# Six banks of batch 1's first DFT stage by sums and differences in a spectral filter with a gated MLP

## The chip, the cores and the metric

The kernel runs on one core of a Trainium2 chip. A core has TensorE (PE in the profile; its weight loads are the row PEld), VectorE (DVE), ScalarE (ACT), GpSimd (POOL) and SyncE (SP), which here only issues DMAs. Sixteen DMA engines move data between HBM and the core's SBUF, whose 128 partitions hold the operands; matmul results go to PSUM, which has eight banks of 128 partitions by 512 fp32 numbers. The metric is the time of one execution on the device in microseconds.

## What is computed

```
x: (8, 3008, 256) fp32     filt: (1505, 256) complex, given as two fp32 arrays
X = rfft(x, axis=1)                      # along the 3008 positions of a batch
y = irfft(X * filt, n=3008, axis=1)      # a global filter
out = (relu(y @ w_gate) * (y @ w_val)) @ w_out
w_gate, w_val: (256, 1536)   w_out: (1536, 256)   out: (24064, 256) fp32
```

The 24,064 tokens are the positions of the eight batches. The MLP is by far the larger part of the arithmetic; the transforms are written as matmuls too.

## The kernel before

**The transform.** A batch's 3008 positions are a grid of 94 (n1) by 32 (n2, here called the columns). The forward transform has two stages. Stage A is a DFT over n1: for each column, 94 input rows times a table of cosines and sines, WA. Stage 2 (`fwd`, L395) is a DFT over the columns, with 64x32 tiles of TensorE side by side. Its result is multiplied by the real and by the imaginary part of the filter (`product`, L411: `tt` with Ftr, `uu` with Fti), and `inv` (L437) transforms back over the columns. A last matmul, `item_c` (L555), goes back over n1 and yields y transposed (psY, then yT in bf16), as the MLP needs it.

**The MLP.** Tokens are worked in 47 blocks of 512. `gv` (L573) makes, for one of 12 slices of the hidden width, the value and the gate by two bf16 matmuls each (psV, psG), ACT copies psV, and DVE forms relu(gate) times value. `o_part` (L591) multiplies by w_out for the block before. The main loop runs over the blocks and slices; the transforms of the later batches are hung onto its steps by hand (`at_step`, L701). The order of work on every engine is the order in which the program is written.

**The prologue.** Before the first gv, batch 0 must be transformed and filtered; `first_b` (L474) does that in steps, and while its DVE and ACT work goes on, stage A of batch 1 fills TensorE. This stage A has 16 banks: each is one fp32 matmul (`a_bank`, L262, shown at L267) of the whole table WA, 128x128, by four columns and one half of the 256 channels, 512 numbers. The fp32 matmul shows as two records in the profile. `a_1` (L282) calls it and has ACT drain the bank: channels' first half (h = 0) in one copy into a part of dCb named AS1[0], the second half (h = 1) in two copies into two buffers with the tag "asb", of which the pool has three. The order of the 16 banks is a plain list: groups p of eight columns, halves h, four columns s within the group (L670). `first_b` takes two of them at each of three stops (`item(2)`), the third just ahead of `inv(0, 2)`, the last part of batch 0's inverse transform over the columns. Then follow in the text: the loads of the MLP's weights, issued by POOL (`load_vg`, L245, `load_o`, L250); the table M1; the two transposes `turn_d` on DVE (L318, shown at L302), which turn batch 0's result into the form that psY reads; `item(7)`; the psY matmuls of the first block; `item(3)`; and the main loop.

**Loads of batch 1.** SP issues twelve DMAs (`load_x`, L187, shown at L192) behind a small one that holds the queue until the filter is there. Each carries 32 (or 30) rows of n1 and eight columns, 8 KB a row. Row i of chunk m goes into partition m + 4 i, so one DMA spreads over all 128 partitions. The columns come in order; XF[0] holds columns 0 to 15, XF[1] 16 to 31.

**Other steps that the text below speaks of.** `store_half` (L323) and `load_half` (L329) send the h = 0 half of stage A's result through HBM, once its last bank is drained; `turn_1` (L309) turns the h = 1 half on DVE. The products of batch 0 are split: for i = 0, 1, 2 and e = 1 POOL makes them, from a copy `xs` that ACT takes out of PSUM (L421, L422), the rest are made by DVE (L424). PSUM banks are handed out from a list in the order in which they were given back (`bank`, L149), so the order of the text decides which bank, and so which wait, a matmul meets. The last POOL operation of the prologue multiplies Fti by plus and minus one (L694).

Of the kernel before, what the change touches and what calls it, by code (L numbers as in the profile page):

```python
# [12 lines left out]
FP32 = mybir.dt.float32  # L13
BF16 = mybir.dt.bfloat16
ALU = mybir.AluOpType
# [14 lines left out]
N1, N2 = 94, 32  # L30
# [86 lines left out]
def kernel(  # L117
# [10 lines left out]
    nc = tc.nc  # L128
# [9 lines left out]
    assert NB * W == B * S  # L138

    wa_h, fold_h, f2_h, tab_h = _tables()  # L140

    ctx.enter_context(tc.manual_schedule())
    consts = ctx.enter_context(tc.tile_pool(name="consts", bufs=1))
# [12 lines left out]
    def done(t):  # L156
        free.append(held.pop(id(t))[0])
# [7 lines left out]
    XF = [consts.tile([128, NX2 * D], FP32, name=f"XF{c}") for c in range(N2 // NX2)]  # L165
    XP = [t[:, i * 2048:i * 2048 + 2048].rearrange("p (k d) -> p k d", d=512) for t in XF for i in range(2)]
    WA = pro.tile([128, 128], FP32)
    AS0 = pro.tile([128, 4, N2 // 2, D // 8, 4], BF16)
    DS0 = AS0.rearrange("p q n c f -> p (q n c f)").rearrange("p (k c f) -> p k c f", c=D // 2, f=4)
    dCb = consts.tile([128, 48, D], BF16)  # L170
# [1 line left out]
    AS1 = [dCb[:, 32:48, :].rearrange("p n d -> p (n d)").rearrange("p (l c d) -> p l c d", l=NC2, d=D // 2)]  # L172
    WF = consts.tile([128, 4, 32], FP32)
    M1 = consts.tile([128, 2, N1], BF16)
    F2 = consts.tile([128, NG, 64], BF16)
    I2t = consts.tile([128, 2, NG // 2, 64], BF16)
    I2u = pro.tile([128, 2, NG // 2, 64], BF16)
# [101 lines left out]
            nc.scalar.copy(dst[:, :, q.start + i], src[:, :, i])  # L279
        done(psA)  # L280

    def a_1(p, s, h):  # L282

        psA = a_bank(NC2 * p + 4 * s, 4, h * D // 2, D // 2)
        if h and len(AS1) == 1:
            for _ in range(2):
                t = sb.tile([128, NC2 * D], BF16, tag="asb", bufs=3, name="asb")
                AS1.append(t.rearrange("p (l c d) -> p l c d", l=NC2, c=N2 // NC2))
        ts = AS1[1:] if h else AS1[:1]
        w = D // 2 // len(ts)  # L290
        for i, t in enumerate(ts):
            nc.scalar.copy(t[:, 4 * s:4 * s + 4, p, :], psA[:, :, i * w:(i + 1) * w])
        done(psA)

    def turn_a(dst, src):

# [66 lines left out]
    def tiled_a(b, j):  # L363

        banks = [bank("psF", 2, D) for _ in range(4)]
        for c in range(4):
            for q in range(4):
                r = 32 * q
                nc.tensor.matmul(banks[q][32 * c:32 * c + 32], WF[r:r + 24, c, :],  # L369
                                 fold[b, j][c][r:r + 24], start=True, stop=True,  # L370
                                 tile_position=(r, 32 * c))
        asf = sb.tile([128, NC2 * D], BF16, tag="asb", bufs=3, name="asb")
        asf = asf.rearrange("p (n q d) -> p n q d", n=2, d=D)
        for q in range(4):
            copy = nc.scalar.copy if q % 2 == 0 else nc.vector.tensor_copy
            copy(asf[:, :, q, :], banks[q])  # L376
            done(banks[q])
        for c in range(4):
            rr = 2 * (1 - c // 2) + c % 2
            nc.sync.dma_start(_ap(Abuf[b], (rr * N2 + 8 * j) * NG * D, [[D, NG], [NG * D, 8], [1, D]]),  # L380
                              asf[32 * c:32 * c + NG].rearrange("p n q d -> p (n q) d"))
# [5 lines left out]
            nc.sync.dma_start(ats[b][:, 8 * z:8 * z + 8].rearrange("p j d -> p (j d)"),  # L387
                              _ap(Abuf[b], 8 * z * D, [[NG * D, 128], [1, 8 * D]]))

    ON_POOL = ((0, 1), (1, 1), (2, 1))  # L390
    ats = {}

    psXs, tus, left, xs = {}, {}, {}, {}
# [43 lines left out]
    def inv(b, q):  # L437

        psD = [bank("psD", 2, D) for c in range(4)]
        last = 0 if b else 1  # L440
        for m in range(2):
            for k in range(last + 1):
                for r in range(2):
                    for c in range(4):
                        for e in range(2):
                            i = 2 * q + m
                            nc.tensor.matmul(psD[c][64 * e:64 * e + 64, m],  # L447
                                             (I2t, I2u)[k][32 * c:32 * c + 32, r, 2 * i + e, :],
                                             tus[b, i, e, k][32 * c:32 * c + 32, r],
                                             start=(k == r == 0), stop=(k == last and r == 1),  # L450
                                             tile_position=(32 * c, 64 * e))
        dst = sb.tile([128, 8, D], BF16, tag="dsb", bufs=3, name="dsb") if b else DS0
        def out(cs):
            for c in cs:
                copy = nc.vector.tensor_copy if (c % 2 if b else (q, c) in ((1, 3), (2, 0), (2, 1))) else nc.scalar.copy
                if b:
                    copy(dst[:, c:8:4, :], psD[c])
                else:
                    k, g = 4 * q + c // 2, c % 2 * 2
                    copy(dst[:, k:k + 3:2, :, g:g + 2], psD[c].rearrange("p m (f e) -> p m e f", f=2))  # L460
                done(psD[c])
        if not b:
            return out(range(4))

        def rest():
            out((2, 3))
            for z in range(4):
                nc.sync.dma_start(_ap(Dbuf[b], (64 * (z // 2) + z % 2) * NG * D + 8 * q * D,
                                      [[2 * NG * D, 32], [1, 8 * D]]),
                                  dst[32 * z:32 * z + 32])  # L470
        out((0, 1))
        return rest

    def first_b(item):  # L474

        def products(i, es=(1, 0)):
            for e in es:
                for k in range(2):
                    product(0, i, e, k, pool=(i, e) in ON_POOL)

        for i in range(3):
            fwd(0, i)
            if i < 2:
                products(i)
        make_back_u()
        products(2)
        warm(3)
        fwd(0, 3)
        products(3, (1,))
        warm(3)  # L490
        fwd(0, 4)
        item(2)
        products(3, (0,))
        inv(0, 0)
        fwd(0, 5)
        products(4)
        item(2)
        products(5)
        place_own()
        inv(0, 1)  # L500
        item(2)
        inv(0, 2)

    dCs = {}
# [161 lines left out]
            warm(4)  # L666
    hold = sb.tile([2, 8], BF16, tag="hold", bufs=1)
    nc.sync.dma_start(hold, Ftr[0:2, 4, 0:8])
    load_x(1, sp, ((0, 0, 2 * q), (0, 2 * q, 4 * q), (1, 0, 2 * q), (1, 2 * q, 4 * q)))
    items = iter([(p, s, h) for p in range(4) for h in range(2) for s in range(2)])  # L670

    def item(n):
        for _ in range(n):
            p, s, h = next(items)
            a_1(p, s, h)
            if (p, s, h) == (3, 1, 0):
                new_at(1)
                store_half(1)
                load_half(1)

    first_b(item)
    load_vg(0, DFF // 2)
    load_vg(DFF // 2, DFF)
    load_o()
    nc.gpsimd.tensor_copy(M1, tabs[:, 578:].rearrange("p (l n) -> p l n", l=2))
    for h in range(2):
        turn_d(h)
    item(7)
    for m in range(y_items(0)):
        for h in range(2):  # L690
            item_c(m, h)
    item(3)
    turn_1(0)
    nc.gpsimd.tensor_scalar(Fti, Fti, conj[:, 0:1], 1.0, op0=ALU.mult, op1=ALU.mult)  # L694
# [90 lines left out]
```

## Time and profile before

| What | Value |
|---|---|
| median of three runs | 865.34 us (863.85, 865.34, 865.4) |
| profiled execution, its own time | 863.39 us |
| its span | 861.6 us |
| PE busy | 853.8 us |
| DVE, ACT, POOL busy | 578.6, 500.2, 458.0 us |
| first gv matmul (psV) | 45.85 us |
| twelve loads of batch 1, issued | 20.84 to 29.89 us |

The busy times are sums over the span of one execution. A row of a timeline gives the start and the length in us, the engine, the line, the operation, the tiles it writes and reads with partitions and sizes, and how many instructions were taken together; in brackets stands the idle time ahead of it and what ended it. The windows give for each stretch of time the busy time and the number of instructions of PE, PEld, DVE, ACT and POOL, then TensorE's granted clock, the busy share of the DMA engines and their GB/s; a share can pass 1 a little, since packets of an engine overlap at their ends. Times of moments are counted from the start of the span.

### The profile page before, as it was taken

The page shows a single profiled execution, that of the slowest core. Times are in us where ns is not written, and L with a number is a line of the kernel's source. Part 1 is how long each engine was busy: PE and PEld are TensorE (multiplying, and loading weights), DVE is VectorE, ACT ScalarE, POOL GpSimd, SP SyncE. Part 2 cuts the span into 40 slices and gives each one's busy share as a digit, 9 for nine tenths or more (in the row PEclk, how much of TensorE's full clock was granted, in tenths as well). Part 3 has the DMA queues.
Part 4 walks back from the last instruction along what each step waited for, and adds up shares of the span by engine and source line. Part 5 has one row for each costly group of instructions (what it writes and reads, how often), then busy time and mean ns, then how long its engine had stood idle before and what let it go on. Part 6 is the DMA issues. An engine that isn't in the chain of part 4 may idle for free.

```text
span 861.6 us, 20366 instructions
## 1 busy us (share of the span) xinstructions
PE 853.8 (99%) x7614; PEld 497.3 (58%) x7614; DVE 578.6 (67%) x864; ACT 500.2 (58%) x944; POOL 458.0 (53%) x494
## 2 busy tenths in 40 slices
PE   9999999999999999999999999999999999999997
PEld 4456655656556555665556665565655656666665
DVE  3878865777657876577765787658766578555554
ACT  5765565556655565555655565655565555565552
POOL 6747890488986765776667756867550033000001
PEclk9999999999999999999999999999999999999999
DMA  9995375333762339534294333842454222511112
GB/s 248 239 166 124 98 156 145 104 113 106 195 190 79 80 92 190 175 84 102 73 211 153 99 101 94 201 147 77 103 118 119 97 62 51 129 39 31 37 32 55
DMA packets 102862, 101.60 MB, mean 118 GB/s; under 512 B 21703, under 2 KB 89959, under 8 KB 101995
## 3 DMA queue, kind: packets, MB, share of 16 engines
q1 hardware_dynamic: 83407, 77.93, 34.1%
q0 software_dynamic: 18848, 21.68, 11.6%
q8 instruction: 60, 0.98, 0.5%
q10 hardware_dynamic: 508, 0.68, 0.3%
q14 instruction: 39, 0.32, 0.1%
HBM read 58.23 MB, written 45.88 MB: 121 GB/s over the span
## 4 chain that ended last, share of the span: by engine, by line
PE 98%; DMA 1%; SPq 1%; issue 0%; ACT 0%; DVE 0%
PE psV L578 29%; PE psO L599 29%; PE psG L578 28%; PE psF L369 3%; PE psA L267 3%; PE psY L561 3%; PE psD L447 2%; PE psX L404 1%; DMA XF<-in_x_dram 1%; SPq L192 1%; PE psI L209 0%; ACT AS L460 0%; DVE XF L608 0%; SPq L637 0%
## 5 line engine op out<-in xcount | busy, mean ns | idle before, releaser
L583 DVE SCALAR_TENSOR_TENSOR prod<-psG,vsb 128x512 bf16<-128x512 f32 x564 | 389.5, 691 | 234.0 <-ACT vsb L581 229.9
L581 ACT CAST vsb<-psV 128x512 bf16<-128x512 f32 x564 | 332.4, 589 | 217.6 <-PE psV L578 210.2
L599 PE MATMUL psO<-WoT,prod 128*128 128x256 bf16 x2256 | 336.5, 273 | 0.0
L578 PE MATMUL psV<-yT,WvT 128*128 128x512 bf16 x1128 | 336.2, 380 | 0.0
L578 PE MATMUL psG<-yT,WgT 128*128 128x512 bf16 x1128 | 335.3, 379 | 0.0
L599 PEld LDWEIGHTS <-prod 128*128 128x128 bf16 x2256 | 220.7, 98 | 143.4
L578 PEld LDWEIGHTS <-WgT 128*128 128x128 bf16 x1128 | 110.0, 97 | 133.9 <-issue 1.1
L434 POOL TENSOR_TENSOR pp<-tt,uu 128x256 bf16<-128x256 f32 x84 | 61.1, 727 | 169.8 <-DVE uu L424 159.9
L578 PEld LDWEIGHTS <-WvT 128*128 128x128 bf16 x1128 | 100.4, 98 | 36.9 <-issue 25.6
L569 ACT CAST yT<-psY 128x470 bf16<-128x470 f32 (+16 forms) x134 | 58.8, 457 | 46.6 <-PE psY L561 46.5
L608 ACT COPY osb<-psO 128x512 f32<-128x512 f32 x92 | 53.9, 586 | 25.2 <-PE psO L599 24.1
L621 POOL DMA_DIRECT2D out_dram<-osb x5 | 2.6, 539 | 119.2 <-ACT osb L608 117.7
L424 DVE TENSOR_TENSOR tt<-psX,Ftr 128x512 f32<-128x512 f32 (+1 forms) x93 | 63.5, 683 | 0.5 <-PE psX L404 0.5
L424 DVE TENSOR_TENSOR uu<-psX,Fti 128x512 f32<-128x512 f32 (+1 forms) x93 | 63.3, 681 | 0.2 <-DMA Fti<-in_filt_i_dram 0.2
L435 POOL TENSOR_TENSOR pp<-tt,uu 128x256 bf16<-128x256 f32 x84 | 61.0, 726 | 0.0
L355 POOL TENSOR_TENSOR fold<-XF 128x1024 f32<-128x1024 f32 x24 | 56.5, 2352 | 4.8 <-DMA XF<-in_x_dram 4.3
L356 POOL TENSOR_TENSOR XF<-XF 128x1024 f32<-128x1024 f32 x24 | 56.5, 2355 | 1.9
L259 POOL CAST scr<-prod 128x8 f32<-128x8 bf16 x19 | 3.6, 192 | 85.7 <-DVE prod L583 85.7
L342 POOL DMA_DIRECT2D XF<-in_x_dram x76 | 45.7, 604 | 2.1 <-issue 1.0
L376 DVE CAST asb<-psF 128x512 bf16<-128x512 f32 x48 | 30.9, 686 | 17.7 <-PE psF L369 17.7
L376 ACT CAST asb<-psF 128x512 bf16<-128x512 f32 x48 | 25.8, 589 | 28.9 <-PE psF L369 28.9
L561 PE MATMUL psY<-M,dCb 96*128 96x94 bf16 (+2 forms) x514 | 39.9, 205 | 0.0
(68 smaller groups left out, 456.4 us busy)
## 6 DMA issues: line engine op xcount, KB each, us to landing
Dbuf<-dsb SPq DMA_DIRECT2D x84, 128.0 KB
dCb<-Dbuf SPq DMA_DIRECT2D x56, 192.0 KB
XF<-in_x_dram POOLq DMA_DIRECT2D x38, 256.0 KB, 7.4
Abuf<-asb SPq DMA_DIRECT2D x96, 96.0 KB
at<-Abuf SPq DMA_DIRECT2D x18, 512.0 KB
XF<-in_x_dram SPq DMA_DIRECT2D x31, 256.0 KB
XF<-in_x_dram POOLq DMA_DIRECT2D x76, 96.0 KB, 5.2
out_dram<-osb SPq DMA_DIRECT2D x69, 94.0 KB
```

What stands on the lines that cost most here:

```text
L355: tt(t, xp[:, 0:2], xp[:, 2:4], op=ALU.add)
L356: tt(xp[:, 2:4], xp[:, 0:2], xp[:, 2:4], op=ALU.subtract)
L376: copy(asf[:, :, q, :], banks[q])
L424: nc.vector.tensor_tensor(p, psX, filt, op=ALU.mult)
L434: nc.gpsimd.tensor_tensor(p[:, 0], tt[:, 0], uu[:, 1], op=ALU.subtract)
L435: nc.gpsimd.tensor_tensor(p[:, 1], tt[:, 1], uu[:, 0], op=ALU.add)
L561: nc.tensor.matmul(psY[:, o:o + w], d_rows(b, col, h), M1[:, 1, n1:n1 + w] if b == 0 else M1[:NROW, 0, n1:n1 + w], start=True, stop=True)
L569: copy(yT[:, h, p:p + w], psY[:, o:o + w])
L578: nc.tensor.matmul(pt[:, :W], w[:, h, ft * 128:(ft + 1) * 128], yT[:, h, y0:y0 + W], start=(h == 0), stop=(h == 1))
L581: nc.scalar.copy(vsb, psV[:, :W])
L583: nc.vector.scalar_tensor_tensor(prod, in0=psG[:, :W], scalar=0.0, in1=vsb, op0=ALU.max, op1=ALU.mult)
L599: nc.tensor.matmul(psO[:, t % 2], prods[ft][:, t * 128:(t + 1) * 128], WoT[:, ft, :], start=(ft == 0), stop=(ft == NFT - 1))
```

## The change

Stage A of batch 1 is done in three ways. Columns 0 to 7 and 24 to 31 stay as they were, eight banks. Columns 8 to 23 are loaded otherwise: four DMAs (`load_halves`) bring them in runs of eight columns, with the rows n1 = 0 to 47 in one half (k = 0) and 47 to 94 in the other (k = 1), columns 8 to 15 into partitions 0 to 47, columns 16 to 23 into partitions 64 to 111. Of those eight banks, six are done from sums and differences: POOL forms row n1 plus row n1 + 47 and row n1 minus row n1 + 47, four adds in all (`fold_halves`), and `a_halves` multiplies the sum by the columns of the table that it needs and the difference by the others, with four fp32 matmuls on four 64x64 tiles for two banks. The last two (`a_halves(1, 1)`) are done without sums, as two accumulating steps over the two halves of n1. A new table WH holds the parts of WA in that arrangement.

With it come smaller ones. The buffers "asb" are four, not three. In `first_b` the products of i = 0, 1, 2 are written with three tt ahead of three uu on DVE, and POOL's in the order tt, tt, uu, uu, tt, uu. The third stop in `first_b` takes one bank, not two; ahead of psY stand `a_halves(1, 1)`, one plain bank and three `a_halves` with sums, and behind it two plain banks, not three. The first plain bank after columns 0 to 7 is one of columns 24 to 27, which come with the last three loads. One AS copy of `inv(0, 1)` moves from ACT to DVE. On POOL the adds, M1 and a small copy of a sign column stand between the halves of the weight loads, and the multiplication of Fti comes after the last of them. On SP there are eleven DMAs for batch 1 instead of twelve: three `load_x`, four `load_halves`, WH, three `load_x`.

```diff
+    wh_h = np.zeros((128, 2, 128), np.float32)
+    n1 = np.arange(N1).reshape(2, N1 // 2)
+    for r in (0, 64):
+        wh_h[r:r + N1 // 2] = wa_h[n1 % 32 * 4 + n1 // 32].transpose(1, 0, 2)
...
-    def a_1(p, s, h):
-
-        psA = a_bank(NC2 * p + 4 * s, 4, h * D // 2, D // 2)
+    def out_1(psA, n2, h):
+
         if h and len(AS1) == 1:
             for _ in range(2):
-                t = sb.tile([128, NC2 * D], BF16, tag="asb", bufs=3, name="asb")
+                t = sb.tile([128, NC2 * D], BF16, tag="asb", bufs=4, name="asb")
...
+    XH = [XF[k][:, NC2 * D * (1 - k):NC2 * D * (2 - k)] for k in range(2)]
+
+    def load_halves(b):
+
+        for k in range(2):
+            for r in range(2):
+                nc.sync.dma_start(XH[k][64 * r:64 * r + 48],
+                                  _ap(x, ((b * N1 + N1 // 2 * k) * N2 + NC2 * (1 + r)) * D,
+                                      [[N2 * D, 48], [1, NC2 * D]]))
+
+    def cols_h(k, s, d0, nd):
+
+        return XH[k].rearrange("p (n d) -> p n d", d=D)[:, 4 * s:4 * s + 4, d0:d0 + nd]
+
+    def fold_halves(s, d0, nd):
+
+        lo, hi = (cols_h(k, s, d0, nd) for k in range(2))
+        t = pro.tile([128, 4, nd], FP32, tag=f"sum{s}", name="sum")
+        nc.gpsimd.tensor_tensor(t, lo, hi, op=ALU.add)
+        nc.gpsimd.tensor_tensor(hi, lo, hi, op=ALU.subtract)
+        for h in range(d0 * 2 // D, (d0 + nd) * 2 // D):
+            sums[s, h] = t[:, :, h * D // 2 - d0:h * D // 2 - d0 + D // 2]
+
+    def a_halves(s, h):
+
+        banks = [bank("psA", 4, D // 2) for _ in range(2)]
+        lo, hi = (cols_h(k, s, h * D // 2, D // 2) for k in range(2))
+        if (s, h) in sums:
+            jobs = [(64 * e, 64, 0, src, True, True) for e, src in ((1, sums[s, h]), (0, hi))]
+        else:
+            jobs = [(0, 128, k, src, k == 0, k == 1) for k, src in enumerate((lo, hi))]
+        for c, w, k, src, start, stop in jobs:
+            for r in (0, 64):
+                nc.tensor.matmul(banks[r // 64][c:c + w], WH[r:r + N1 // 2, k, c:c + w], src[r:r + N1 // 2],
+                                 start=start, stop=stop, tile_position=(r, c))
+        for r in range(2):
+            out_1(banks[r], NC2 * (1 + r) + 4 * s, h)
...
-                copy = nc.vector.tensor_copy if (c % 2 if b else (q, c) in ((1, 3), (2, 0), (2, 1))) else nc.scalar.copy
+                copy = nc.vector.tensor_copy if (c % 2 if b else (q, c) in ((1, 2), (1, 3), (2, 0), (2, 1))) else nc.scalar.copy
...
         for i in range(3):
             fwd(0, i)
-            if i < 2:
-                products(i)
+        for k in range(2):
+            for i in range(2):
+                product(0, i, 1, k, pool=True)
+        for i in range(3):
+            product(0, i, 0, 0)
         make_back_u()
-        products(2)
+        for k in range(2):
+            product(0, 2, 1, k, pool=True)
+        for i in range(3):
+            product(0, i, 0, 1)
...
-        item(2)
+        item(1)
         inv(0, 2)
...
-    load_x(1, sp, ((0, 0, 2 * q), (0, 2 * q, 4 * q), (1, 0, 2 * q), (1, 2 * q, 4 * q)))
-    items = iter([(p, s, h) for p in range(4) for h in range(2) for s in range(2)])
+    load_x(1, sp, ((0, 0, 2 * q),))
+    load_halves(1)
+    nc.sync.dma_start(WH, nc.inline_tensor(wh_h, name="dft_wh").ap())
+    load_x(1, sp, ((1, 2 * q, 4 * q),))
+    items = iter([(n2, h) for p in (0, 3) for h in range(2) for n2 in (NC2 * p, NC2 * p + 4)])
...
     first_b(item)
     load_vg(0, DFF // 2)
+    fold_halves(0, 0, D)
+    nc.gpsimd.tensor_copy(M1, tabs[:, 578:].rearrange("p (l n) -> p l n", l=2))
+    nc.gpsimd.tensor_copy(sign, conj[:, 0:1])
+    fold_halves(1, 0, D // 2)
     load_vg(DFF // 2, DFF)
     load_o()
-    nc.gpsimd.tensor_copy(M1, tabs[:, 578:].rearrange("p (l n) -> p l n", l=2))
+    nc.gpsimd.tensor_scalar(Fti, Fti, sign, 1.0, op0=ALU.mult, op1=ALU.mult)
     for h in range(2):
         turn_d(h)
-    item(7)
+    a_halves(1, 1)
+    item(1)
+    for s, h in ((0, 0), (0, 1), (1, 0)):
+        a_halves(s, h)
+    new_at(1)
+    store_half(1)
+    load_half(1)
     for m in range(y_items(0)):
         for h in range(2):
             item_c(m, h)
-    item(3)
+    item(2)
     turn_1(0)
-    nc.gpsimd.tensor_scalar(Fti, Fti, conj[:, 0:1], 1.0, op0=ALU.mult, op1=ALU.mult)
```

More of the change, by code (lines that the diff above doesn't have):

```diff
@@ L167 @@
     WA = pro.tile([128, 128], FP32)
+    WH = pro.tile([128, 2, 128], FP32)
     AS0 = pro.tile([128, 4, N2 // 2, D // 8, 4], BF16)
@@ L174 @@
     M1 = consts.tile([128, 2, N1], BF16)
+    sign = consts.tile([128, 1], BF16)
     F2 = consts.tile([128, NG, 64], BF16)
@@ L290, in a_1 @@
         w = D // 2 // len(ts)
+        l, p = n2 % NC2, n2 // NC2
         for i, t in enumerate(ts):
-            nc.scalar.copy(t[:, 4 * s:4 * s + 4, p, :], psA[:, :, i * w:(i + 1) * w])
+            nc.scalar.copy(t[:, l:l + 4, p, :], psA[:, :, i * w:(i + 1) * w])
         done(psA)
+    def a_1(n2, h):
+        out_1(a_bank(n2, 4, h * D // 2, D // 2), n2, h)
+    XH = [XF[k][:, NC2 * D * (1 - k):NC2 * D * (2 - k)] for k in range(2)]
[5 more added lines that the diff above has]
+                                      [[N2 * D, 48], [1, NC2 * D]]))
+    sums = {}
+    def cols_h(k, s, d0, nd):
[20 more added lines that the diff above has]
+            out_1(banks[r], NC2 * (1 + r) + 4 * s, h)
     def turn_a(dst, src):
@@ L371, in tiled_a @@
                                  tile_position=(r, 32 * c))
-        asf = sb.tile([128, NC2 * D], BF16, tag="asb", bufs=3, name="asb")
+        asf = sb.tile([128, NC2 * D], BF16, tag="asb", bufs=4, name="asb")
         asf = asf.rearrange("p (n q d) -> p n q d", n=2, d=D)
@@ L388, in load_at_tiled @@
                               _ap(Abuf[b], 8 * z * D, [[NG * D, 128], [1, 8 * D]]))
-    ON_POOL = ((0, 1), (1, 1), (2, 1))
     ats = {}
@@ L478, in products @@
                 for k in range(2):
-                    product(0, i, e, k, pool=(i, e) in ON_POOL)
+                    product(0, i, e, k)
         for i in range(3):
             fwd(0, i)
-            if i < 2:
-                products(i)
+        for k in range(2):
[3 more added lines that the diff above has]
+            product(0, i, 0, 0)
         make_back_u()
-        products(2)
+        for k in range(2):
+            product(0, 2, 1, k, pool=True)
+        for i in range(3):
+            product(0, i, 0, 1)
         warm(3)
@@ L668 @@
     nc.sync.dma_start(hold, Ftr[0:2, 4, 0:8])
-    load_x(1, sp, ((0, 0, 2 * q), (0, 2 * q, 4 * q), (1, 0, 2 * q), (1, 2 * q, 4 * q)))
-    items = iter([(p, s, h) for p in range(4) for h in range(2) for s in range(2)])
+    load_x(1, sp, ((0, 0, 2 * q),))
[3 more added lines that the diff above has]
+    items = iter([(n2, h) for p in (0, 3) for h in range(2) for n2 in (NC2 * p, NC2 * p + 4)])
     def item(n):
         for _ in range(n):
[L674 to L679, printed above, removed]
+            a_1(*next(items))
     first_b(item)
     load_vg(0, DFF // 2)
+    fold_halves(0, 0, D)
+    nc.gpsimd.tensor_copy(M1, tabs[:, 578:].rearrange("p (l n) -> p l n", l=2))
+    nc.gpsimd.tensor_copy(sign, conj[:, 0:1])
+    fold_halves(1, 0, D // 2)
     load_vg(DFF // 2, DFF)
     load_o()
-    nc.gpsimd.tensor_copy(M1, tabs[:, 578:].rearrange("p (l n) -> p l n", l=2))
+    nc.gpsimd.tensor_scalar(Fti, Fti, sign, 1.0, op0=ALU.mult, op1=ALU.mult)
     for h in range(2):
         turn_d(h)
-    item(7)
+    a_halves(1, 1)
[5 more added lines that the diff above has]
+    load_half(1)
     for m in range(y_items(0)):
```

## The prediction

> **What bounds the kernel now.** I read the shares and slices of the page first, then the chain that ended last, then the timelines of PE, DVE, ACT and POOL for the first 54 us, and last the DMA share of single stretches.
>
> ```profile
> span 861.6 us, 20366 instructions
> PE 853.8 (99%) x7614; PEld 497.3 (58%) x7614; DVE 578.6 (67%) x864; ACT 500.2 (58%) x944; POOL 458.0 (53%) x494
> PEclk9999999999999999999999999999999999999999
> PE 98%; DMA 1%; SPq 1%; issue 0%; ACT 0%; DVE 0%
> ```
>
> TensorE is the bound: it works 99% of the span at the full granted clock, and the chain that ended last is nearly all PE. From the first gv matmul on (psV, L578, 45.85 us) its timeline has no gap, and the diff leaves the order of work behind that point as it is. So the whole question is when gv starts. PE's timeline ahead of it:
>
> ```profile
> 25.82 0.42 PE L404 MATMUL psX<-at,F 64*32 64x256 bf16 x16
> 26.93 1.96 PE L267 MATMUL psA<-XF,WA 128*128 128x512 f32 x4 [0.68 <-DMA XF<-in_x_dram]
> 30.55 1.98 PE L267 MATMUL psA<-XF,WA 128*128 128x512 f32 x4 [0.31 <-ACT AS L460]
> 33.48 1.99 PE L267 MATMUL psA<-XF,WA 128*128 128x512 f32 x4
> 35.39 0.42 PE L447 MATMUL psD<-tt,I2t 32*64 32x256 bf16 x16
> 36.40 6.28 PE L267 MATMUL psA<-XF,WA 128*128 128x512 f32 x14
> 42.66 0.70 PE L561 MATMUL psY<-M,dCb 128*128 128x94 bf16 x12
> 43.20 2.81 PE L267 MATMUL psA<-XF,WA 128*128 128x512 f32 x6
> 45.85 0.59 PE L578 MATMUL psV<-yT,WvT 128*128 128x512 bf16 x2
> ```
>
> The L267 rows are the 16 banks of stage A of batch 1, each two records of an fp32 matmul: 7 banks in 42.66 - 36.40 less a switch are about 0.86 us each. PE looks continuous, but another chain ends at the same place, on VectorE:
>
> ```profile
> 36.49 1.29 DVE L460 CAST AS<-psD 128x512 bf16<-128x512 f32 x2 [1.94 <-PE psD L447]
> 37.89 4.72 DVE L302 STREAM_TRANSPOSE dCb<-AS 128x2048 f32<-128x2048 f32 x2
> ```
>
> The two transposes of turn_d end at 42.61, and psY, which reads them, starts at 42.66. DVE had waited 1.94 us for inv(0,2). From the start of inv(0,2) (35.39) to the end of the transposes are 7.22 us that no cut of PE's work shortens. Bound now: PE, with turn_d 0.05 us behind it.
>
> **Part 1: sums and differences on PE.** Six banks, 6 x 0.86 = 5.15 us, become three a_halves of two 64x64 fp32 tiles at four places. That the places run side by side is shown by the tiled group of later batches: psF L369, 16 tiles and 32 records, takes 1.07 us in the chain, two passes and a switch. Three such groups cost 3 x 0.86 plus a switch, about 2.75 us. The two banks by halves without sums go as two passes over pairs of tiles, 1.73 us, what they cost now. PE's work falls by about 2.4 us.
>
> **Part 2: which part counts.** One bank fewer stands before inv(0,2) (its third stop has one item for two): -0.86. Against it, the new order of the products on POOL and DVE lets fwd(0,4) take other buffers: its first matmul now waits for the third xs copy on ACT, which ends at 26.68, so it starts near 26.90 in place of 25.82, and the first stop at 27.25 in place of 26.93: +0.32. inv(0,2) then starts at 35.39 - 0.86 + 0.32 = 34.86 (rounded from the rows), turn_d ends 7.22 later, 42.08, and psY starts at 42.13 (-0.53). PE itself would be ready at 41.6, so half of what part 1 frees becomes a wait for turn_d. After psY there are two banks for three: another -0.86. gv then starts at 45.85 - 1.39 = 44.46.
>
> **Part 3: POOL.** It now makes the sums. A 128x1024 f32 add takes 2.35 us (fold, L355), a 512 one half of that; two of each are 7.1 us, put between the two halves of the weights. POOL is free for them at 32.95, after two weight issues:
>
> ```profile
> 31.41 0.79 POOL L247 DMA_DIRECT2D WvT<-in_moe_w_val_dram  x1
> 32.20 0.73 POOL L247 DMA_DIRECT2D WgT<-in_moe_w_gate_dram  x1
> 36.38 2.82 POOL L694 TENSOR_SCALAR Fti<-Fti,tabs 128x3072 bf16<-128x3072 bf16 x1
> ```
>
> The first pair ends at 37.65 with (0,0) due on PE at 38.6, the second at 40.5 with (1,0) due at 40.4. Free while turn_d, ending 42.08, stays the later one: the cover is about 0.5 us. Behind them the second half of Wv and Wg is issued at 40.5 to 42 for 32.9 to 34.4 now, and Wo after it; at about 2 us a transfer they land by 46 and 50.6. gv needs the former at its seventh step (near 49.6) and Wo at 56: covers of 3.5 us and more. The sign product on Fti (2.82) goes last on POOL; its next work before was at 53.32.
>
> **Part 4: ACT and DVE.** ACT drains psA. In PE's 4.4 us from 36 it now gets 8 banks for 5, at 0.5 to 0.7 each. I count it through to dCb at 43.1 and yT at 43.8, 0.6 ahead of gv at 44.46. DVE takes one AS copy (0.65) from ACT in its 1.94 us wait: nothing. Three tt then three uu hide the 0.20 us that uu waited for Fti; worth 0 at gv, as turn_d's start is set by inv(0,2). The fourth asb buffer removes no wait that the trace shows: 0. Store and reload of batch 1's half start 1.7 us earlier than L326's 44.94 and now beside the weights; the reload landed at 56.5 for a use at 60.6, a cover of 4 us.
>
> **Part 5: SP, the one wait that may cost.** The third stop's single item is now column 24 and needs the last three loads; before, that place needed the sixth at most, down since 29.4. It is due at 33.80. SP's queue holds three loads (770 KB), four long runs (1.57 MB into partitions 0 to 47 and 64 to 111), WH (0.13), three loads (0.77): 3.24 MB for 3.08. The first three landed at 26.79 and the nine behind them (2.31 MB) at 33.60, 0.34 MB/us. At that pace the last is down at 26.79 + 2.47 / 0.34 = 34.1, 0.3 late, and with 0.14 from landing to start 0.43. Everything behind, turn_d too, moves by it. The bounds come from what the DMA engines gave in single stretches (columns: DMA share, then GB/s, at the end):
>
> ```profile
> 30.00:31.00 1.00, 0.69 (x17) 0.30 (x2) 1.00 (x3) 1.00 (x3) 0.94 (x2) 1.00 1.03 426
> 31.00:32.00 1.00, 1.00 (x4) 0.38 (x2) 1.00 (x2) 1.00 (x3) 1.00 (x3) 1.00 1.01 377
> 70.00:71.00 1.00, 1.00 (x8) 0.68 (x7) 0.82 (x3) 0.81 (x2) 0.87 (x2) 1.00 0.71 235
> 118.00:122.00 4.00, 4.00 (x55) 1.99 (x53) 2.71 (x5) 3.08 (x6) 3.84 (x3) 1.00 1.14 209
> 122.00:126.00 4.00, 4.00 (x56) 1.92 (x54) 2.03 (x3) 1.63 (x3) 3.84 (x4) 1.00 1.17 182
> ```
>
> The first two are the x loads, whose rows lie every fourth partition; the last two are mostly dCb<-Dbuf, into 48 neighbouring partitions as the long runs are, and there busy engines move half as much. 70 to 71 lies between: x into 24 neighbouring partitions, engines not full. At 0.4 MB/us nothing is late (delay 0). At 195 KB/us the long runs alone take 8.1 us; with 0.9 MB behind at 0.34 the last load is down at 37.5, delay 3.9. I take 0.43: the same queue, source and 8 KB pieces as the loads now; the slow rows have pieces of 512 bytes.
>
> [...] The stretches say 209 and 182 for neighbouring partitions against 426 and 377 for spread ones. [...]
>
> **Sum.** -0.53 - 0.86 + 0.43 = -0.96 against the profiled execution's 863.39 (span 861.6 and 1.8 around it): 862.4. That execution lies 1.95 under the median of the runs, 865.34; on the median's scale 864.3.
>
> **Rivals.** *Slow long runs* (slower): the mechanism of part 5 with the last two rows as pace. Price: delay 2.5 (235 KB/us) to 3.9 (195), net +1.1 to +2.5: 866.4 to 867.8. It turns the sign where the last load lands past 35.0, a pace under 281 KB/us. For it the two rows of full engines at half the rate; against it the piece size and that 24 neighbouring partitions gave 235 with engines 71% busy.
> *PE's cut counts in full*: if turn_d were through by 41.6, gv would start 0.5 to 1.0 earlier: net -1.9 to -2.4, 862.9 to 863.4. Against it the 7.22 us of DVE that nothing shortens.
> *A new wait in the groups*: if the 64x64 tiles go two at a time, three groups at 1.73 add 2.6 to PE, of which turn_d's wait hides 0.5: net +1.1, 866.4. If they go one at a time, four passes each, it is 7.7 more and net +6.2, 871.5. POOL's adds, fed 2 us late, would push (1,0) and psY to 43.6, net +0.5. Against it psF's 1.07 for 16 tiles and fold's even 2.35.
> *Nothing gained*, the delay eating just the 1.39, lies between forecast and first rival and is counted in them.
>
> **Numbers.** 0.2% (1.7 us) is about what a measurement of this kernel can tell from no change; the runs before lie 1.55 apart. Forecast 0.48 (863.6 to 865.0; 0.17 of it faster than the bound, as the runs' spread and the hand count could add 0.8, 0.31 within), slow long runs 0.29 (0.09 of it within, 0.20 slower), PE in full 0.09 (faster), a new wait 0.14 (0.10 slower, 0.04 within). Faster 0.26, same 0.44, slower 0.30. Range 862.8 to 867.9: from PE in full to just past the slow runs' price; the forecast's own range is 863.6 to 865.0.
>
> **What would show it.** Right: the third stop's PE row (two records) waits no more than 0.5 us on DMA XF, near 34; one psA group of short rows per a_halves, about 0.9 apart; psY waits half a us on DVE dCb L302's row; gv's first psV near 44.9. Wrong: a wait of 2 us or more on XF at the third stop with DMA share 1 at some 200 GB/s from 27 to 36; a_halves rows 1.7 us apart; POOL's adds starting after 34, or PE waiting for them; psV waiting for yT from ACT.

## The result: 0.84% slower

The changed kernel takes 871.83 us (median of six runs, 869.49 to 873.78), the kernel before, measured beside it, 864.79. The ratio is 1.0084 with an interval of 1.0068 to 1.0101, so about 7 us are lost where 1 us was forecast to be gained. The profiled execution took 870.7 us; its span is 868.6 against 861.6.

The shares and the chain of the page, after the change:

```profile
span 868.6 us, 20408 instructions
PE 855.8 (99%) x7630; PEld 497.6 (57%) x7630; DVE 578.7 (67%) x865; ACT 499.3 (57%) x943; POOL 464.5 (53%) x499
PEclk9799999999999999999999999999999999999999
PE 95%; DMA 3%; DVE 1%; SPq 1%; issue 0%; DVEq 0%
```

PE's busy time rose by 2 us although six banks of work became three groups, the clock row has a 7 in its second slice, and DMA holds 3% of the chain for 1%. The timeline of PE says where:

```profile
29.95 3.75 PE L273 MATMUL psA<-XF,WA 128*128 128x512 f32 x4 [2.45 <-DMA XF<-in_x_dram]
35.48 1.98 PE L273 MATMUL psA<-XF,WA 128*128 128x512 f32 x4 [0.32 <-ACT AS L509]
40.67 2.00 PE L273 MATMUL psA<-XF,WA 128*128 128x512 f32 x2 [2.20 <-DMA XF<-in_x_dram]
42.61 0.65 PE L496 MATMUL psD<-tt,I2t 32*64 32x256 bf16 x16
47.31 0.65 PE L340 MATMUL psA<-sum,WH 47*64 47x512 f32 x2
47.32 0.65 PE L340 MATMUL psA<-XF,WH 47*64 47x512 f32 x2
50.39 0.71 PE L616 MATMUL psY<-M,dCb 128*128 128x94 bf16 x12 [0.28 <-DVE dCb L352]
50.94 1.95 PE L273 MATMUL psA<-XF,WA 128*128 128x512 f32 x4
52.72 0.59 PE L633 MATMUL psV<-yT,WvT 128*128 128x512 bf16 x2
```

The first stop (29.95) waits 2.45 us for its load and then takes 3.75 us for two banks, twice as long as before. The third stop is at 40.67, when the last load of batch 1 is down, and its one bank takes 2.00. The first psV starts at 52.72 instead of 45.85, 6.87 later, and behind it lie 868.6 - 52.72 = 815.9 us, as before (861.6 - 45.85 = 815.75). In this execution the whole loss stands ahead of the first psV. The groups with sums are what was hoped: 47.31 and 47.32 are two tile rows side by side.

The windows of the same time, after the change (columns: the stretch, its length, the five engines' busy time, granted clock, DMA share, GB/s):

```profile
27.00:30.00 3.00, 0.55 (x18) 0.16 (x17) 3.00 (x6) 0.00 (x0) 3.00 (x4) 0.51 1.00 158
30.00:33.00 3.00, 3.00 (x4) 1.09 (x4) 1.54 (x3) 0.59 (x1) 2.73 (x5) 0.50 0.96 161
42.00:45.00 3.00, 3.00 (x69) 1.80 (x70) 0.56 (x1) 1.06 (x2) 2.92 (x5) 0.64 0.09 17
```

From 27 to 33 us the DMA engines are fully busy and move 160 GB/s; before, 30 to 32 us had 377 to 426. In the trace's packets the 8 KB pieces that start between 26 and 32 us last 755 to 863 ns (medians of two-microsecond stretches); before, 309. The granted clock is half from 27.07 to 33.90 us and from 40.73 to 44.14 us, which is why the rows there are twice as long. (The first drop came 0.4 us before the wait for the load began, behind a gap of 1.72 us ahead of 25.97; what ended that gap the profile does not show.)

### The profile page after: what moved, and what is told of

The parts are those of the page before. It is cut to its first block, busy times and chain, and to the rows that moved or that the text cites. A ratio compares the mean times of both kernels' runs of the same rounds, so it can differ in the third digit from the quotient of the medians.

```text
span 868.6 us, 20408 instructions
## 1 busy us (share of the span) xinstructions
PE 855.8 (99%) x7630; PEld 497.6 (57%) x7630; DVE 578.7 (67%) x865; ACT 499.3 (57%) x943; POOL 464.5 (53%) x499
## 4 chain that ended last, share of the span: by engine, by line
PE 95%; DMA 3%; DVE 1%; SPq 1%; issue 0%; DVEq 0%
PE psV L633 29%; PE psO L654 28%; PE psG L633 28%; PE psF L419 3%; PE psY L616 3%; DMA XF<-in_x_dram 3%; PE psA L273 2%; PE psD L496 2%; PE psX L453 1%; DVE dCb L352 1%; SPq L198 0%; DVE AS L509 0%; PE psI L215 0%; DVE XF L663 0%; SPq L692 0%
```

## The experiments

Each is read by the start of the first psV, by what lies behind it in the span, and by its time. SP's first load of batch 1 went out between 20.7 and 22.0 us in these executions, since the loads ahead of it vary; so much of a difference between two single profiles means nothing.

### Rows into both halves of the partitions, one transfer for both groups of columns

```diff
-            for r in range(2):
-                nc.sync.dma_start(XH[k][64 * r:64 * r + 48],
-                                  _ap(x, ((b * N1 + N1 // 2 * k) * N2 + NC2 * (1 + r)) * D,
-                                      [[N2 * D, 48], [1, NC2 * D]]))
+            for p, step, i, n in ((0, 2, 0, 32), (1, 4, 32, 16)):
+                nc.sync.dma_start(XH[k][p:128:step],
+                                  _ap(x, ((b * N1 + N1 // 2 * k + i) * N2 + NC2) * D,
+                                      [[NC2 * D, 2], [N2 * D, n], [1, NC2 * D]]))
```

> The changed kernel with one thing undone in effect: the long runs of columns 8 to 23 go into partitions of both halves of the 128 in every DMA (64 rows on every second partition, then 32 rows on every fourth), the same bytes, rows and 8 KB pieces; the table WH is laid out to match. Theory, the partitions: the neighbouring partitions 0 to 47 or 64 to 111 made pieces of 309 ns last 600 to 1000 ns, so the pieces return to about 309 to 400 ns, the last of batch 1's loads lands by about 34.5 us instead of 40.5, the third stop waits under 0.6 us for it, the granted clock stays at 1.0, and the first psV starts at about 44.9 us (45.85 before the change, 52.72 after): about 1 us faster than before, 863.8 us. Rival, the order of the queue and the number of bytes: the last loads stay late whatever the partitions, first psV at 51 to 53 us, 870 to 872 us. Rival, the rest of the change (sums, POOL, DVE order): first psV at 46 us or later with the loads on time.

It took 893.23 us, ratio 1.0324 (1.0299 to 1.0349), the first psV at 76.29. The third stop in PE's timeline and one window of this run:

```profile
64.08 2.04 PE L274 MATMUL psA<-XF,WA 128*128 128x512 f32 x2 [29.38 <-DMA XF<-in_x_dram]
```

```profile
44.00:62.00 18.00, 0.00 (x0) 0.00 (x0) 0.00 (x0) 0.00 (x0) 0.00 (x0) 0.50 0.13 50
```

For 18 us the DMA share is 0.13, the work of two of sixteen engines (0.13 x 16 = 2.1), at 50 GB/s, and the pieces last the undisturbed 309 ns. The source is written with an outermost dimension of size 2, which these loads have in no other run; why that leaves the other engines idle the trace does not show. The run says nothing about partitions; it changed something else with them.

### Warm-up matmuls at the third stop

```diff
         inv(0, 1)
+        warm(10)
         item(1)
```

> The changed kernel with ten warm-up matmuls of 0.21 us (512 columns each, result unused) ahead of the third stop, where TensorE waits 2.2 us for the last load. Theory, the clock: the idle stretch costs twice, by the wait and by the lower granted clock behind it (0.64 from 42 to 45 us), which lengthens the third stop and inv(0,2) from 1.06 us of one bank to 1.94 and inv(0,2) by about 0.4 us. With the matmuls in the gap the clock stays near 1 there, and the first psV starts about 1.2 us earlier than 52.72, at 51.5 us: about 870.6 us. Rival, the clock is only a sign of the wait: first psV at 52.7 us or later.

The time is 872.82 us, 1.0087 (1.0063 to 1.0111): no gain. The profile shows why a time alone misleads here. From the third stop to the first psV are 10.40 us (38.70 to 49.10) against 12.05 in the changed kernel (40.67 to 52.72), so the lower clock behind the wait costs 1.65 us and the matmuls take that away. But in this execution the last load was also down 2 us earlier, and the first psV at 49.10 led to a new wait, in PE's timeline:

```profile
67.93 0.63 PE L453 MATMUL psX<-at,F 64*32 64x256 bf16 x31 [3.76 <-DMA at<-Abuf]
```

Behind the first psV lie 821.6 us, not 815.8: 3.76 of waiting and some 2 us at a granted clock of 0.63 from 68 to 72 us. Batch 1's reload, which the prediction had counted as covered by 4 us, is late.

### The long runs last in the queue

```diff
     load_x(1, sp, ((0, 0, 2 * q),))
+    load_x(1, sp, ((1, 2 * q, 4 * q),))
     load_halves(1)
     nc.sync.dma_start(WH, nc.inline_tensor(wh_h, name="dft_wh").ap())
-    load_x(1, sp, ((1, 2 * q, 4 * q),))
```

> The changed kernel with the four long runs and WH moved behind the last three loads in the queue, still into neighbouring partitions. Theory, the partitions are slow and everything that shares the queue with them or stands behind them is late: the first three loads land at about 26.8 us again and the last plain one by about 29.5, the third stop waits for no load (starts near 33.8 us), and the long runs land at about 37.5 us. POOL's adds then end at about 44.7 us and become what psY waits for; first psV near 47.8 us, 866.7 us. Rival, the bytes or the number of pieces make the stretch slow, not the partitions: the long runs land by 34 us and the first psV starts at 45 us.

The stops came as the theory has them: first at 27.29, third at 33.86, without a wait for a load. The long runs were down at 37.5 us, the figure expected, where the rival said 34. The pieces of the six plain loads last about 309 ns, those of the long runs about 590. The first psV is at 51.13, not 47.8: TensorE waited from 36 to 37.85 for the table WH, which stands behind the long runs in the queue, and ran at a clock of 0.50 to 0.61 until 48. Then came the wait for the reload (2.9 us; 820.7 behind). 878.87 us, 1.0153 (1.0105 to 1.0202). The four executions lie between 873.97 and 882.87 us and the profiled one is the fastest; what the others lost beyond it is not shown.

### The kernel before, with the long runs alone

```diff
-    load_x(1, sp, ((0, 0, 2 * q), (0, 2 * q, 4 * q), (1, 0, 2 * q), (1, 2 * q, 4 * q)))
+    load_x(1, sp, ((0, 0, 2 * q),))
+    for k in range(2):
+        for r in range(2):
+            nc.sync.dma_start(XF[k][64 * r:64 * r + 48, NC2 * D * (1 - k):NC2 * D * (2 - k)],
+                              _ap(x, ((N1 + N1 // 2 * k) * N2 + NC2 * (1 + r)) * D,
+                                  [[N2 * D, 48], [1, NC2 * D]]))
+    load_x(1, sp, ((1, 2 * q, 4 * q),))
```

> The kernel before with only its loads of columns 8 to 23 changed: four long runs into partitions 0 to 47 and 64 to 111 in the order of the changed kernel, nothing else (those columns are then in the wrong rows for its matmuls, so the result is not the reference's). Theory, the loads alone carry the loss: the first stop waits for its load until about 29.9 us and runs at half clock, as in the changed kernel, so the third stop starts about 5 us later than 33.48, and the first psV at about 50.8 us: 869.7 us. Rival, the new work on POOL, DVE and ACT carries a good part: first psV under 48 us.

The first psV is at 48.60 and the time 866.32 us, 1.0017 (1.0003 to 1.0032). The first stop ran at half clock here too (3.65 us), yet only 2.75 us are lost. The expectation of 50.8 was too high: it carried the changed kernel's worse first stop over. But the order matters as well. The kernel before works on columns 8 to 23 next and asks for the last loads only with the seventh bank behind inv(0,2), near 41.6 us; the changed kernel's third stop asks for them ahead of inv(0,2), in front of the 7.22 us chain of turn_d.

### The long runs on every second partition

```diff
-                nc.sync.dma_start(XH[k][64 * r:64 * r + 48],
+                nc.sync.dma_start(XH[k][r:r + 95:2],
```

> The changed kernel with the four long runs written to every second of the partitions 0 to 95 instead of 0 to 47 and 64 to 111: same source rows, same number of transfers and rows, same 8 KB pieces, split alike over the engines; only the partitions differ (the rows then lie wrong for the matmuls, so the result is not the reference's). Theory, the partitions: pieces last 309 to 400 ns in place of 600 to 1000, the last of batch 1's loads lands by 35.5 us instead of 40.5, the first stop runs at full clock, and the first psV starts at 45 to 46 us. Rival, anything else about the queue (order, bytes, 48 rows a transfer): pieces stay at 450 ns and more and the first psV starts later than 48 us. The time is then 864 to 865 us, unless batch 1's reload (at<-Abuf) collides with the weights that POOL now issues later: then TensorE waits for it once, near 66 us, by 2 us or more, and the time is 867 to 870 us with the first psV unchanged.

Nothing but the partitions differs, and the first psV moves from 52.72 to 47.40, though not to 45 or 46. It lies ahead of all six profiles of the changed kernel (49.69 to 53.21, the other five below). The windows from 26 to 34 us show the order, first in the changed kernel:

```profile
26.00:30.00 4.00, 1.55 (x21) 0.49 (x21) 4.00 (x8) 0.56 (x2) 4.00 (x5) 0.63 1.07 170
30.00:34.00 4.00, 4.00 (x28) 1.44 (x35) 1.54 (x3) 0.85 (x2) 2.73 (x5) 0.51 0.99 172
```

And on every second partition of 0 to 95:

```profile
26.00:30.00 4.00, 3.17 (x39) 1.24 (x45) 4.00 (x7) 1.49 (x4) 4.00 (x5) 1.00 0.96 270
30.00:34.00 4.00, 3.69 (x112) 1.77 (x103) 4.00 (x8) 3.54 (x9) 2.95 (x5) 1.00 1.02 248
```

The engines are as busy, and move half as much again; the clock stays at 1.00. Pieces last 397 to 532 ns, between the theory's 309 to 400 and the rival's 450 and more, so this spread is not yet that of the loads before. The run still took 871.07 us, 1.0078 (1.0052 to 1.0105), for the earlier psV again met the reload: 3.23 us of waiting, 821.0 us behind. The rest of the gain was given back there.

### The weights early again: three runs

```diff
     load_vg(0, DFF // 2)
+    load_vg(DFF // 2, DFF)
+    load_o()
     fold_halves(0, 0, D)
...
     fold_halves(1, 0, D // 2)
-    load_vg(DFF // 2, DFF)
-    load_o()
```

In the run with warm-up matmuls:

> The run with warm-up matmuls again, with POOL issuing the second half of the weights and Wo ahead of its adds, as in the kernel before (POOL is idle there from 33 to 38 us). Theory, the late weights: in the run with warm-up matmuls the reload of batch 1's half landed at 65 us, among the weights, and TensorE waited 3.8 us for it and ran below full clock behind; with the weights early that wait is gone and the span behind the first psV is the 815.8 us of the kernel before instead of 821.6, so the time falls from 872.8 to about 867 us. Price to watch: the weights share the engines with the last x loads, which may land 1 us later. Rival, the reload is late for another reason: the wait near 68 us stays.

In the run with every second partition:

> Both at once: long runs on every second partition (result not the reference's) and all weights issued ahead of POOL's adds. Theory, partitions and late weights are the two causes of the loss and the rest of the change is worth what was forecast: first psV at 44.9 to 45.5 us, no wait on at<-Abuf, 815.8 us behind it, 863 to 864 us, about 1 us faster than before. Rival, the sums on POOL and the buffers cost time of their own: first psV after 46 us.

In the changed kernel, nothing else:

> The changed kernel with only the order on POOL undone: second half of the weights and Wo ahead of the adds. Theory, late weights make batch 1's reload late in part of the executions of the changed kernel: the first psV stays near 51 to 53 us, as the long runs are slow as before, no wait for at<-Abuf, and the time is 868.5 to 870.5 us with less scatter than 869.5 to 873.8. Rival, the order on POOL does not matter: 871 to 873 us.

None of the three waits for at<-Abuf, and each has 815.8 or 815.9 us behind its first psV. With warm-up matmuls 868.17 us, 1.0040 (1.0024 to 1.0055), psV at 51.39. With every second partition 865.92 us, 1.0004 (0.9979 to 1.0029), psV at 48.31: not the 44.9 to 45.5 of the theory, since the third stop still waits 2.33 us for its load. The changed kernel with this one order undone takes 867.50 us, 1.0034 (1.0012 to 1.0055), psV at 49.83, better than was expected of it: of 0.84% about 0.5 goes with the order on POOL. How much of that is the missing wait is not shown: against the changed kernel's profile the gain lies ahead of psV (49.83 for 52.72), and both have 815.9 us behind it. Nor do the warm-up matmuls show a gain in any time (868.17 with them, 867.50 without).

The wait itself shows in two executions with nearly the same first psV. SP's queue in the changed kernel with the wait (psV at 49.69, the fifth of the profiles below), then with the weights early (49.83):

```profile
48.66 1.64 SPq L376 DMA_DIRECT2D Abuf<-dCb  x4
54.94 4.92 SPq L382 DMA_DIRECT2D at<-Abuf  x4
```

```profile
48.80 2.67 SPq L376 DMA_DIRECT2D Abuf<-dCb  x4
51.64 3.58 SPq L382 DMA_DIRECT2D at<-Abuf  x4
```

The reload is issued when the store is down, 6.3 us after it with late weights and 2.8 with early ones. Late weights alone don't make the wait. In the four profiles that have it (warm-up matmuls, every second partition and the long runs last, all with late weights, and the fifth below) the store is issued 2.2 to 2.4 us after POOL's issue of Wo, and the reload 5.9 to 6.5 us after the store. In the six with late weights and no wait the store is 4.0 to 5.3 us behind Wo, the reload 5.1 to 5.8 behind the store. Why these 2 us decide is open.

### The order of the products alone

```diff
         for i in range(3):
             fwd(0, i)
-            if i < 2:
-                products(i)
+        for k in range(2):
+            for i in range(2):
+                product(0, i, 1, k, pool=True)
+        for i in range(3):
+            product(0, i, 0, 0)
         make_back_u()
-        products(2)
+        for k in range(2):
+            product(0, 2, 1, k, pool=True)
+        for i in range(3):
+            product(0, i, 0, 1)
```

> The kernel before with only the new order of batch 0's products (three tt ahead of three uu on DVE; tt, tt, uu, uu, tt, uu on POOL). By the prediction's part 2 the fourth fwd waits for the third xs copy, so the first stop moves from 26.93 to about 27.25 us and the first psV from 45.85 to about 46.2 us. Rival, the order is free or gains the 0.2 us of the wait for Fti: first psV at 45.6 to 45.9 us.

```profile
26.95 0.42 PE L404 MATMUL psX<-at,F 64*32 64x256 bf16 x16 [1.12 <-ACT xs L421]
27.30 1.98 PE L267 MATMUL psA<-XF,WA 128*128 128x512 f32 x4
46.18 0.59 PE L584 MATMUL psV<-yT,WvT 128*128 128x512 bf16 x2
```

The fourth fwd waits for the third xs copy, the first stop is at 27.30 and the first psV at 46.18: 0.33 us lost, on the spot foreseen. It is one execution (863.71 us); the time can't tell 0.3 us.

### Gaps within one half, in eight and in twelve transfers

```diff
+            for p, step, i, n in ((0, 2, 0, 32), (1, 4, 32, 16)):
+                for r in (0, 64):
+                    nc.sync.dma_start(XH[k][r + p:r + 64:step],
+                                      _ap(x, ((b * N1 + N1 // 2 * k + i) * N2 + NC2 * (1 + r // 64)) * D,
+                                          [[N2 * D, n], [1, NC2 * D]]))
```

> The changed kernel with weights ahead of POOL's adds and the long runs in other partitions of the same half: per half of n1 and group of columns 32 rows on every second partition of 0 to 63 (or 64 to 127) and 16 rows on every fourth; WH is laid out to match, so the result is the reference's. Eight transfers for four, the same bytes and pieces. Theory, half of the partitions: a transfer that stays within 0 to 63 or 64 to 127 is slow wherever its rows lie there; pieces stay at 450 to 600 ns, the last load lands at 38 to 40.5 us, first psV 49.5 to 52 us. Rival, neighbouring partitions are the trouble: as with every second partition of 0 to 95, pieces of 320 to 360 ns, last load near 36.6 us, first psV 47.5 to 48.3 us, about 866 us.

Pieces last 490 to 560 ns, the last load was down at 39.5 us and the first psV at 50.07: the figures of the theory that one half of the partitions is slow wherever the rows lie in it. 867.11 us, 1.0014 (0.9993 to 1.0035), not to be told from the 867.50 of neighbouring partitions. The run is not clean: SP's last three loads went out only at 31.9 us behind more transfers, and the weights were on the engines by then.

> As the run before it, but with the rows in twelve transfers of 16 (every fourth partition of one half, one piece for each engine), the two halves of the partitions in turn. If the two halves can be written at the same time once the engines drift apart, pieces fall under 400 ns, the last load lands by 36 us and the first psV starts by 47.5 us, about 865 to 866 us; if not, it is as with eight transfers, 49.5 to 52 us. SP issues 19 transfers at about 0.55 us, ending near 31.5 us, so the issue alone doesn't set the landing.

Twelve transfers were worse: SP issued the last loads from 32.45 us, the DMA share fell to 0.65 from 26 to 30 us and 0.77 from 30 to 32 for want of issued work, the third stop waited 6.85 us, psV came at 53.01. 872.17 us, 1.0084 (1.0062 to 1.0105). It does not decide whether two halves can be written at once.

### The rows of the kernel before, in the changed kernel

```diff
-    load_halves(1)
+    load_x(1, sp, ((0, 2 * q, 4 * q), (1, 0, 2 * q)))
```

with the weights early.

> The changed kernel with weights ahead of POOL's adds and columns 8 to 23 loaded as in the kernel before: six transfers of 32 (or 30) rows of 8 KB, row i of a chunk in partition m + 4 i (the rows lie wrong for the halves, so the result is not the reference's). Everything else is the changed kernel. Theory, the layout of the long runs and the late weights are the whole loss: pieces last 309 ns again, the third stop waits less than 0.6 us, the first psV starts at 44.5 to 45.3 us (less or more by what the loads start earlier or later than 20.84), no wait on at<-Abuf, 815.8 us behind it: 0.5 to 1.3 us faster than before, near 863.6 us. Rival, transfers of 48 rows have no part in it and the loads are late for their place in the queue: the third stop waits 1.5 us or more, first psV after 46.5 us.

It takes 865.07 us, 0.9997 (0.9978 to 1.0015). Pieces last 309 ns again and the first stop runs at full clock. In the profiled execution the loads began 1.15 us later than in the kernel before (21.99 against 20.84), and the first psV is at 47.95, 2.1 us later. Two waits stand in PE's way:

```profile
36.35 1.10 PE L273 MATMUL psA<-XF,WA 128*128 128x512 f32 x2 [1.41 <-ACT AS L509]
44.61 1.07 PE L340 MATMUL psA<-XF,WH 47*64 47x512 f32 x4 [0.21 <-POOL XF L326]
45.62 0.71 PE L616 MATMUL psY<-M,dCb 128*128 128x94 bf16 x12
```

The first names ACT, but in the run with the long runs last the same matmul started at 33.86, ahead of that copy (33.95), so it is not tied to it; the last load was down at 36.15, with the weights beside it since 34 us. The second is the price of the early weights: POOL's adds start only at 36.76, behind 3.1 us more of weight issues, and end at 44.56, and psY starts at 45.62, while turn_d was through at 44.37. So the loss goes with layout and order. With the weights early the times order the layouts: 867.50 us for neighbouring partitions, 867.11 for gaps within one half, 865.92 for every second partition, 865.07 for the rows of the kernel before. A gain cannot be told from none; the interval would hold the 1 us forecast too.

### Five more profiles of the changed kernel

> The changed kernel, unaltered, profiled once more. Theory, two terms that trade with each other: where the long runs land early (first psV before 51 us), the reload meets the late weights, TensorE waits 2 to 4 us for at<-Abuf and the span behind the first psV is about 821 us; where they land late (first psV near 52.7 us), there is no such wait and 815.8 us behind it. Rival: the span behind the first psV is 815.8 us in every execution and the loss is all in the start of the first psV.

> The changed kernel once more, as the look before it: first psV before 51 us goes with a wait for at<-Abuf and about 821 us behind it, first psV near 52.7 us with none and 815.8 us.

> The changed kernel once more. If its profiled execution takes over 872 us, theory: it holds a wait of TensorE for at<-Abuf of 2 to 4 us and about 821 us behind the first psV; rival: no such wait, and the first psV later than 54 us.

> The changed kernel, another look: over 872 us with a wait of TensorE for at<-Abuf (theory) or with the first psV later than 54 us (rival); under 871 us without that wait.

> The changed kernel, the last look: over 872 us with a wait of TensorE for at<-Abuf (theory) or with the first psV later than 54 us (rival); under 871 us without that wait.

| execution | time, us | first psV | store issued after Wo | wait for at<-Abuf | behind psV |
|---|---|---|---|---|---|
| first | 868.91 | 50.97 | 4.0 | none | 815.8 |
| second | 869.10 | 51.12 | 5.0 | none | 815.9 |
| third | 870.17 | 52.22 | 5.3 | none | 815.8 |
| fourth | 871.18 | 53.21 | 5.1 | none | 815.9 |
| fifth | 872.92 | 49.69 | 2.4 | 3.3 | 821.1 |

The first misses the limit of 51 us that its theory had set for the wait. The fifth, the earliest psV, is the slowest. Its list of PE's waits and its timeline:

```profile
PE psX L453 <- DMA at<-Abuf: 3.3, 1, 3.3
```

```profile
49.69 0.59 PE L633 MATMUL psV<-yT,WvT 128*128 128x512 bf16 x2
68.05 0.63 PE L453 MATMUL psX<-at,F 64*32 64x256 bf16 x31 [3.30 <-DMA at<-Abuf]
```

So the changed kernel loses in one of two ways: either the long runs are so slow that psV starts 5.1 to 7.4 us late, or they are less so, psV starts 3.8 us late, and the store and reload come so soon behind the late weights that they cost another 5. The timed executions near 873 us fit the second way; only one such execution was profiled.

## Why the prediction was wrong

**The step that failed** is part 5, "I take 0.43: the same queue, source and 8 KB pieces as the loads now". The pieces kept source, size and queue, and lasted two to three times as long for the partitions they went to. The third stop came at 40.67 instead of 34.23 (33.80 and the 0.43), 6.44 us later: a delay of 6.87 us for 0.43, above the range of delays as well, whose end was 3.9. The rows of 209 and 182 GB/s that I set aside for their 512-byte pieces were the near ones; in the changed kernel the stretch had 158 to 172.

Counted by landings, the four long runs came down between 29.81 and 37.82 us, 8.0 us for the 4.6 that 1.57 MB take at 0.34 MB/us: 3.4 of the 6.44. The other 3.0 are the first three loads, down at 29.81 instead of 26.79; part 5 held their landing fixed. The loads behind the long runs took 2.7 us, as forecast.

Its mechanism stood among the rivals as *slow long runs*, at 0.29 and with +1.1 to +2.5 us. It was priced too low for two reasons. Its slower bound gave the long runs 8.1 us, which is what they took, but nothing for the loads ahead of them, which they held up by 3.0. And the term for the clock was missing: the clock halved again at 40.73 us behind the wait, and from the third stop to the first psV took 12.05 us for the 10.66 forecast. At full clock the same way took 10.40 to 10.42 in five executions (four variants and the fifth profile), so the forecast's own working of that way was right to a quarter of a microsecond. The sum: 6.44 for the load, 1.65 for the clock, less 0.26 that the forecast had too much, is 7.83; and 52.72 - 44.89, the forecast's own psV, is 7.83.

**Part 3 and part 4 failed too**, in part of the executions: no wait for the weights shows, as "covers of 3.5 us and more" had it, but the store and the reload were given "a cover of 4 us" although they now ran "beside the weights". POOL issued these at 45 to 48 us, not from 40.5, because its adds waited for the long runs. The term, 4.9 to 5.8 us where it falls, was in no case of the forecast. The order on POOL is worth about 0.5% of the 0.84.

**Which partitions.** The stretch from 26 to 34 us, its first part shared with the first plain loads, gives 170 and 172 GB/s with the long runs in neighbouring partitions of one half (244 and 206 in the execution with early weights), 264 and 207 with gaps in one half, 270 and 248 on every second partition of 0 to 95, and 305 and 346 with the rows of the kernel before, at a DMA share of 0.91 to 1.07 in all of them. So one half of the partitions was slower than the rows before in every one of them. Touching both halves is not enough for the pace of the rows before: every second partition of 0 to 95 does so, and its pieces still lasted 400 to 530 ns for 309. The execution with early weights does not tell neighbours from gaps in one half (206 against 207). What it is in the partitions that sets the pace no trace here shows, nor the cause of the scatter: from 26 to 32 us the same loads in neighbouring partitions had pieces with medians of 574 to 795 ns from one execution to the next. Why they vary so is open.

**What held.** Part 1: a group with sums takes 0.86 us (48.22 to 49.08 are two passes of 0.43). The halves without sums took 1.9 for the 1.73 forecast. Part 2: +0.32 for the new order, measured alone as +0.33 in one profile, and turn_d as what psY waits for, 0.28 us in the changed kernel. ACT and the fourth buffer caused no wait at gv. The rival *a new wait in the groups* did not occur as far as the tiles go; POOL's adds were late only behind late loads or early weights. The gain of 1 us did not show even with the old rows: in that profile 1.4 us went to a last load still late for its new place at the third stop (the loads had begun 1.15 us later), and 1.25 to POOL's adds behind the early weights. Weights late, the reload is hit; weights early, the adds are late; POOL has not the room for both that part 3 gave it.

## What to carry to other kernels

A layout that a matmul wants (rows in neighbouring partitions) is paid for by the DMA that fills it: before moving a load, compare its pieces' duration in the trace with those of transfers into the same shape of partitions, not with those of the same size (here 755 to 863 ns came for 309). When a load is late, look at what the engine that waits for it issues afterwards, other loads above all, and count the granted clock behind the wait as part of its price (1.65 us here). And read the start of the steady part and the span behind it as two numbers: an edit that gained 5 us in the first gave all of it back in the second, and the time showed nothing.

## What was not expected of the hardware

- Transfers whose source has an outermost dimension of size 2 went at 50 GB/s and a DMA share of 0.13, the work of two of the sixteen engines, and TensorE waited 29.4 us for them in the one run that has them.
- The granted clock changed on a grid in the changed kernel's trace: half from 27.07 us for 6.83, full for 6.83, half from 40.73 for 3.41, all whole multiples of 3.41 us. Cut into stretches of 3.41 us from 23.66 on, TensorE was busy in the first six for 1.69, 0.97, 3.41, 3.09, 1.22 and 3.41 us. Behind the three with 1.69 us and less came one at half clock, behind the three with 3.09 and more one at full clock. At the first stop, waits of 0.9 to 2.6 us, with shorter gaps ahead of them, went with a halved clock in nine executions (two banks in 3.4 to 3.75 us), while gaps of 0.86, 0.38 and 1.14 us in one execution and of 1.51 and 0.31 in another left it at 1.0 (1.96 and 1.95 us). What decides between such cases is not shown here.
- The first three loads of batch 1, whose rows lie spread as before, were down 3 us later in the changed kernel (29.8 for 26.8 us), with the slow transfers queued behind them; with the plain loads behind them they were down at 26.5.
